# New inputs for a kernel's list planner: weight casts further behind landing, later weight parts, smaller transfer times, new tile offsets

## The chip, the cores and the metric

The kernel runs on one core of one Trainium2 chip. The metric is device time in microseconds, the median of several runs. The engines are called as the profile calls them: PE (TensorE matmul; PEld its weight loads), DVE (VectorE), ACT (ScalarE), POOL (GpSimd) and SP (SyncE, which here only issues DMAs).

## The reference

Retention-like attention for 8 batches, 8 heads, 576 positions and 64 values a head, then a mixture of 8 experts over its 4608 rows of 512 values, with a noisy gate that sends each row to two experts:

```python
scores = scale * np.matmul(q, k.transpose(0, 1, 3, 2))
ret = scores * Dmat[None]                      # gamma ** (i - j) for i >= j, else 0
x = np.matmul(ret, v)                          # then (B * S, H * D) = (4608, 512)
noisy_logits = x @ w_gate + np.log1p(np.exp(x @ w_noise)) * noise
top2 = np.argpartition(-noisy_logits, 2, axis=1)[:, :2]   # weights: softmax of the two
for e in range(8):
    for k in range(2):
        mask = top2[:, k] == e
        h = np.maximum(x[mask] @ w1[e], 0.0)   # 512 -> 1024
        out[mask] += top2_w[mask, k, None] * (h @ w2[e])   # 1024 -> 512
```

## The kernel before

**Attention** is worked in 16 units `u` (batch pairs `bp = u // 4`). After each batch pair `route` computes the gate, ranks the rows of each expert and builds a table of row numbers (`xi`), and the pair's rows are written to `xd` in DRAM.

**Expert tiles.** The rows of an expert come in groups `j` of 128, 9.5 groups for each. `tiles` makes 30 tiles `i`, each an expert `e`, a few groups `js`, and the batch pair `bp` after which it can be gathered. Tiles 0 to 10 are *early*: expert 0 to 3's first groups, gathered while attention still runs, up to 256 rows wide. Tiles 11 to 29 are *late* (`bp` is 3) and up to 512 rows wide: one for expert 0, two each for experts 1 to 3, three each for experts 4 to 7.

A tile passes through these operations:

- `fetch`: POOL gathers its rows from `xd` (L1246, `at="fetch1"`); the rows are transposed, late ones by DMA transposes that SP issues (L1258, `fetch2`), early ones and those of expert 3 by PE (L1268, `fetch3`) with a copy from PSUM on ACT or DVE (`fetch4`).
- `up` (early, L1328) or `wide` (late, L1354): x @ w1 on PE, and relus on ACT or DVE (L1337, L1339; `up1`, `wide1`, `wide2`).
- `down`: h @ w2 on PE (L1418 full groups, L1437 half groups). For late tiles these matmuls are put between those of the next tile's `wide`. The last tile's come after all else: the half group in one piece (`record2`), the full group in two columns (L1427, `record3`).
- `finish`: an eviction scaled by the gate (L1469, L1471, L1473; `finish2`, for the split last group `finish1`), then POOL scatters to `out`: rows whose first contribution it is (`finish3`, `first`), or that add to an earlier one (`finish4`, `second`; L1483). A few late groups read the earlier sum beforehand (`before`, L1514).

**Weights.** Expert 0 to 2's are loaded and cast to bf16 by POOL's DMAs. Expert 3 to 7's come in eight parts each (`part`): SP loads 512 KB of f32 into a `big` buffer (L1183, L1186), of which the planner allows this use four at a time, and ACT or DVE casts it to bf16 (helper line L459 or L461). `weights(e + 4)` is called in the last tile of expert `e`; it appends eight parts to a list, the k-th due `SPREAD[e] * k` steps later. A step is one of the eight blocks of a `wide`, so a late tile has eight steps. `due` takes parts from the front of the list only, so a part waits for all before it.

**What sets the order.** Each engine and queue runs its instructions in the order in which `Plan.run` emits them. `Plan` is a list planner: it gives every operation a start time from its own table of costs (`cost` on the engine, `dma` for a transfer, `hold` for a distance behind the landing of a DMA that the operation reads), and emits next the one with

```python
key = (round(t * 20), o.prio, o.i)
```

the smallest. So a priority decides only between operations that could start in the same twentieth of a planned microsecond; the smaller number goes first. Attention's operations have priorities of about `u` (up to some 17), tile `i` has `100 + 4 * i` (late gathers and transposes 8 less), expert 3's parts 60. To that, `op` adds an offset by the operation's name `at`:

```python
prio += ORDER[at][min(3, int(max(0.0, prio)) // 4) if prio < 60 else 4 if prio < 136 else 5]
```

Columns 0 to 3 of `ORDER` are attention's; column 4 is that of tiles 0 to 8 and expert 3's parts, column 5 that of everything later. The planned times are not used on the chip: there every instruction waits for what it reads.

Of the kernel before, what the change touches and what calls it, by code (L numbers as in the profile page):

```python
# [21 lines left out]
F = 1024  # L22
# [5 lines left out]
NH = E * HPE  # L28
FIRST = (1216, 1024, 855, 690, 526, 361, 197, 0)
WAIT = (10, 15, 15)  # L30
SPREAD = (0, 0, 0, 0, 3, 3, 4, 4)
PACE = 2.343
REST = (85.0, 200.0, 1.6)
AHEAD = (2, 3)
# [122 lines left out]
    "route48": (-0.5, -0.25, -1.5, 0, -0.5, -0.5),  # L157
    "route49": (2, 5, 0.5, -1.5, 2, 2),
    "route50": (-2.5, -2, -2, -6.5, -2.5, -2.5),
    "overflow_table1": (-2, -2, -2, -2, -2, -2),  # L160
    "overflow_table2": (-2, -2, -2, -2, -2, -2),
    "overflow_table3": (-0.25, -0.25, -0.25, -0.25, -0.25, -0.25),
    "overflow_table4": (-2, -2, -2, -2, -2, -2),
    "weights1": (-0.75, -0.75, -0.75, -0.75, -0.75, -0.75),
    "part1": (2, 2, 2, 2, 2, 2),
    "fetch1": (-5, -5, -5, -5, -6, -4),
    "fetch2": (-1.25, -1.25, -1.25, -1.25, -1.5, -2.25),
    "fetch3": (0.5, 0.5, 0.5, 0.5, -3, 1.5),
    "fetch4": (-0.25, -0.25, -0.25, -0.25, 0.75, 0.75),
    "fetch5": (0, 0, 0, 0, 0, -4),  # L170
    "fetch6": (-4, -4, -4, -4, -8.25, -1.5),
    "fetch7": (-1.25, -1.25, -1.25, -1.25, 6.5, -3.25),
    "fetch8": (-2.5, -2.5, -2.5, -2.5, -4, 0),
    "mix1": (0.25, 0.25, 0.25, 0.25, 0.25, 0.25),
    "mix2": (4, 4, 4, 4, 4, 4),
    "mix3": (2.25, 2.25, 2.25, 2.25, 2.25, 2.25),
    "up1": (2, 2, 2, 2, 2, 2),
    "wide1": (2.75, 2.75, 2.75, 2.75, 2.75, 2.75),
    "wide2": (1.25, 1.25, 1.25, 1.25, 1.25, 1.25),
    "finish1": (-2.25, -2.25, -2.25, -2.25, -2.25, -2.25),  # L180
    "finish2": (0, 0, 0, 0, 0, 5.5),
    "finish3": (5.75, 5.75, 5.75, 5.75, 24, 6.75),
    "finish4": (5.5, 5.5, 5.5, 5.5, 5.5, 5.5),
    "record1": (3, 3, 3, 3, 3, 3),
    "record2": (1.75, 1.75, 1.75, 1.75, 1.75, 1.75),
    "record3": (6.5, 6.5, 6.5, 6.5, 6.5, 6.5),
    "record4": (2, 2, 2, 2, 2, 2),
}
BIG = 1.0e6
NOV = NCOL * E  # L190
# [223 lines left out]
class Kernel:  # L414
# [762 lines left out]
    def part(self, e, k, prio, after):  # L1177
        pl, nc = self.pl, self.nc
        w, t = self.W[e], pl.buf("big", "exp")

        def ld(_):
            if k < KD:
                nc.sync.dma_start(out=t.t, in_=self.w1[e, k * P:(k + 1) * P, :])  # L1183
            else:
                fo = 2 * (k - KD)
                nc.sync.dma_start(out=t.t.rearrange("p (fo d) -> p fo d", fo=2),  # L1186
                                  in_=self.w2[e, fo * P:(fo + 2) * P, :].rearrange("(fo fi) d -> fi fo d", fi=P))
        pl.op("SP", 0.55, ld, w=[t], prio=prio, dma=1.35, after=after)
        pl.op({"ACT": 1.06, "DVE": 0.7}, 0, lambda g: self.copy(g, w.t[:, k * F:(k + 1) * F], t.t), hold=1,
              r=[t], w=[(w, k)], prio=prio, at="part1")  # L1190

    def tiles(self):
# [35 lines left out]
    def fetch(self, i, t, prio):  # L1228

        pl, nc = self.pl, self.nc  # L1230
        e, js, early = t
        ident = self.fixed["ident"]
        xi = self.fixed[f"xi{early}"]
# [3 lines left out]
        for x, j, two in zip(xg, js, joint):  # L1237
            if two:
                if e % 2:
                    continue  # L1240
                self.tailx[e] = x
            h, n = HPE * e + j, P
            pace = PACE if early == 3 and i > self.ne else 0.0

            def get(_, x=x, h=h, n=n, pace=pace):
                ins = nc.gpsimd.indirect_dma_start(  # L1246
                    out=x.t[:n, :], out_offset=None, in_=self.xd[:rows, :], in_offset=IOff(ap=xi.t[:n, h:h + 1], axis=0),
                    bounds_check=rows - 1, oob_is_err=False)
                if pace:
                    self.tc.add_manual_dep(ins.ins, self.mm.ins.name, mybir.DependencyInfo(  # L1250
                        mybir.DependencyClass.Sync, mybir.DependencyReason.DATA), reason="gathers go at TensorE's pace")
            self.got = pl.op("POOL", 1.3, get, r=[xi if two else (xi, "m")] + self.xd_done[early], w=[x], prio=prio, dma=0.4, pace=pace, slack=3, ind=True, at="fetch1")
        xT = pl.buf("half" if early < 3 else "big", "xt")
        w, m, off = sum(self.size(j) for j in js), len(js) * P, self.off(js)
        xv = lambda m=m: xT.t.bitcast(BF16)[:, :KD * m].rearrange("p (k s) -> p k s", k=KD)
        if early == 3 and e != 3:
            for s, x in enumerate(xg):
                pl.op("SP", 2.0, lambda _, s=s, x=x, n=self.size(js[s]), p=self.span(e, js[s]): nc.sync.dma_start_transpose(  # L1258
                    out=xv()[:, :, off[s]:off[s] + n], in_=x.t[p, :DM // 2].bitcast(BF16)),
                    r=[x], w=[(xT, s)], prio=prio, dma=1.1, hold=3, at="fetch2")  # L1260
        for c in range(0, 0 if early == 3 and e != 3 else len(js), 2):
            p = self.psum("xt")
            pv = lambda p=p: p.t.bitcast(BF16).rearrange("p (k s) -> p k s", k=KD)
# [10 lines left out]
        for x, j, two in zip(xg, js, joint):  # L1274
            k = self.kind(e, j)
            pay = lambda x=x: x.t[:, DM // 2:]
            if early == 3 and two and e % 2 and e < 2:
                c = pl.buf("pay", "exp")
                pl.op("DVE", 0.1, lambda _, x=x, c=c: self.nc.vector.tensor_copy(c.t[:HD], x.t[HD:, DM // 2:DM // 2 + 3]),
                      r=[x], w=[c], prio=prio, hold=3, at="fetch5")  # L1280
                pay, x = (lambda c=c: c.t), c
# [4 lines left out]
            else:  # L1286
                gm, im = self.fix(f"gm{e}", [P, 1]), self.fix(f"im{e}", [P, 2], I32)
                m, mb = self.mix(e)
# [158 lines left out]
    def finish(self, i, t, s, prio, split=False):  # L1447
# [43 lines left out]
        if first:  # L1491
            key = self.outk.setdefault(e, pl.fix())
            self.scats.setdefault(i, []).append(pl.op("POOL", 1.3, lambda _: scat(first, False), r=[y] + src, w=[(key, j)],
                                                      prio=prio, dma=0.76, ind=True, at="finish3"))
        if second:
            rd = [self.outk[x] for x in self.outk if x < e]
            self.scats.setdefault(i, []).append(pl.op("POOL", 1.3 if held else 1.8, lambda _: scat(second, not held),
                                                      r=[y] + src + rd, prio=prio, dma=0.9, after=self.reads if held else (), ind=True, at="finish4"))

    def before_it(self, e):  # L1500
        return [w for x in range(e) for w in self.firsts[x]]
# [1 line left out]
    def before(self, i, t, s, prio):  # L1503

        pl, nc, tc = self.pl, self.nc, self.tc
        e, js, _ = t
        q = self.span(e, js[s], 2)
        if self.size(js[s]) < P:
            q, e = slice(0, P), E - 1
        g, first, second, src = self.t[i]["gi"][s]  # L1510
        y = pl.buf("half", "ty")

        def get(_):
            ins = nc.gpsimd.indirect_dma_start(  # L1514
                out=y.t[q, :], out_offset=None, in_=self.out[:, :], in_offset=IOff(ap=second()[q], axis=0),
                bounds_check=N - 1, oob_is_err=False).ins
            tc.declare_no_dep(ins, group="scat", keep=self.before_it(e), reason="rows of out are disjoint or ordered by hand")
            tc.add_to_no_dep_group("scat", ins)
        self.reads.append(pl.op("POOL", 1.3, get, r=[src] + [self.outk[x] for x in self.outk if x < e], w=[y], prio=prio - 2, dma=0.9))
        self.t[i].setdefault("y", {})[s] = y  # L1520


# [226 lines left out]
```

## Time and profile before

| | |
|---|---|
| time, median of 3 runs | 411.0 us (410.47 to 411.59) |
| profiled execution | 412.69 us, span 411.1 us, granted clock 0.989 |
| busy: PE, ACT, POOL, DVE | 377.1, 272.3, 291.0, 148.2 us |
| DMA | 98.06 MB, mean 239 GB/s |
| gathers, transposes by DMA, scatters | 76, 55, 82 |

The span runs from the first to the last instruction of one profiled execution. A row of the timeline names start, duration, engine, line, operation, output and inputs, and in brackets how long the engine had been idle before it and what ended that. "issue" means that it waited for nothing that the profile shows. In the table of stretches each row has the length and then the busy time of PE, PEld, DVE, ACT and POOL, the granted clock of PE, the share of the DMA engines and GB/s. PE runs attention and the first early tiles up to about 149 us, the other early tiles to about 200 us, and the late tiles from there to 405.7 us.

### The profile page before, as it was taken

To read this page: it belongs to the slowest core of one execution; us is meant where nothing else is said; L and a number is where in the kernel's file an instruction comes from. 1 tells how busy PE (TensorE), PEld (TensorE's weight loads), DVE (VectorE), ACT (ScalarE), POOL (GpSimd) and SP (SyncE) were. 2 spreads that over 40 slices of the span, in tenths; PEclk is the share of its full clock that TensorE was granted. 3 is DMA by queue.
4 is the path that set the end of the run, shared out by engine and by line. 5 is a ranking of instruction groups with operands and counts; after the bars stand their busy time and mean duration, and the time that the engine had idled before them with its cause. 6 is when DMAs were issued, how large, how long until landed. Compare 5 with 4: busy or idle time off the path is not lost.

```text
span 411.1 us, 11031 instructions
## 1 busy us (share of the span) xinstructions
PE 377.1 (92%) x4320; PEld 233.3 (57%) x4320; DVE 148.2 (36%) x413; ACT 272.3 (66%) x468; POOL 291.0 (71%) x379
## 2 busy tenths in 40 slices
PE   4998867889898898999999999999999999999994
PEld 2567656677575666767556554544554454454453
DVE  8456798788269587220111322101011000000002
ACT  2589978898787765776555877666686445555451
POOL 8676783990799848778676477778675776728564
PEclk9899999989999999999999999999999999999999
DMA  8999998999999989999989899999999998839766
GB/s 226 290 298 255 317 305 254 306 269 252 275 286 205 264 188 284 395 246 221 280 188 377 288 331 223 260 251 230 296 257 211 165 202 152 164 45 133 127 94 131
DMA packets 106184, 98.06 MB, mean 239 GB/s; under 512 B 40975, under 2 KB 83472, under 8 KB 106130
## 3 DMA queue, kind: packets, MB, share of 16 engines
q1 hardware_dynamic: 85858, 60.92, 56.0%
q0 software_dynamic: 17584, 36.24, 43.4%
q8 instruction: 34, 0.56, 0.6%
q10 hardware_dynamic: 2688, 0.18, 0.4%
q14 instruction: 20, 0.16, 0.2%
HBM read 73.11 MB, written 26.10 MB: 241 GB/s over the span
## 4 chain that ended last, share of the span: by engine, by line
PE 65%; DVE 8%; POOL 7%; DMA 6%; issue 6%; ACT 6%; POOLq 0%; SPq 0%; another core or an unknown queue 0%; DVEq 0%; ACTq 0%
PE ps L1418 25%; PE ps L1354 23%; PE ps L1328 6%; POOL out_dram L1483 4%; DMA xd<-xg 2%; ACT half L459 2%; DMA half<-in_v_dram 2%; DVE half L783 2%; PE ps L1437 2%; PE ps L808 2%; PE ps L467 1%; POOL half L721 1%; ACT xT L459 1%; DVE olo L1074 1%; PE ps L1268 1%
## 5 line engine op out<-in xcount | busy, mean ns | idle before, releaser
L1337 ACT ACTIVATE half<-ps 128x512 bf16<-128x512 f32 (+5 forms) x184 | 90.6, 503 | 87.5 <-PE ps L1354 55.0
L1418 PE MATMUL ps<-W,half 128*128 128x512 bf16 x432 | 137.8, 379 | 1.4 <-issue 1.1
L1354 PE MATMUL ps<-big,W 128*128 128x512 bf16 (+4 forms) x448 | 124.5, 326 | 0.6 <-DVE half L1473 0.6
L1246 POOL DMA_INDIRECT xg<-xd,xi x76 | 79.1, 1040 | 48.2 <-DMA half<-in_v_dram 11.7
L1483 POOL DMA_INDIRECT out_dram<-half,xg x71 | 90.3, 1272 | 30.1 <-issue 14.8
L1418 PEld LDWEIGHTS <-half 128*128 128x128 bf16 x568 | 54.5, 98 | 62.8 <-issue 3.1
L1354 PEld LDWEIGHTS <-W 128*128 128x128 bf16 x448 | 43.8, 98 | 33.4 <-issue 0.8
L1354 PE MATMUL ps<-big,xT 128*128 128x512 bf16 (+2 forms) x160 | 47.6, 337 | 0.0
L1471 ACT ACTIVATE half<-ps,xg 128x512 f32<-128x512 f32 (+1 forms) x58 | 39.3, 678 | 10.0 <-PE ps L1418 6.7
L783 DVE TENSOR_TENSOR half<-ps,mask 128x512 bf16<-128x512 f32 x64 | 40.3, 682 | 14.3 <-PE ps L775 10.9
L1418 PE MATMUL ps<-xT,half 128*128 128x512 bf16 x136 | 44.9, 379 | 0.0
L459 ACT ACTIVATE half<-ps 128x1024 bf16<-128x1024 bf16 (+1 forms) x42 | 38.5, 946 | 7.9 <-PE ps L744 4.0
L1473 DVE TENSOR_SCALAR half<-ps,xg 128x512 f32<-128x512 f32 (+1 forms) x17 | 10.6, 623 | 76.8 <-PE ps L1437 42.0
L1328 PE MATMUL ps<-half,W 128*128 128x256 bf16 (+1 forms) x288 | 29.1, 255 | 1.6 <-DVE half L461 0.8
L1339 DVE TENSOR_SCALAR half<-ps 128x512 bf16<-128x512 f32 (+5 forms) x12 | 6.8, 569 | 60.5 <-issue 32.9
L1328 PEld LDWEIGHTS <-W 128*128 128x128 bf16 x288 | 23.7, 98 | 5.8 <-issue 1.8
L467 PE MATMUL ps<-mask,ident__61 128*128 128x512 bf16 x68 | 20.3, 429 | 3.7 <-DVE hpf L527 3.7
L1469 DVE SCALAR_TENSOR_TENSOR half<-ps,xg,half 64x256 f32<-64x256 f32 (+2 forms) x7 | 3.6, 521 | 55.2 <-PE ps L1437 32.4
L1354 PEld LDWEIGHTS <-xT 128*128 128x128 bf16 x160 | 15.6, 98 | 12.8 <-issue 0.4
L459 ACT ACTIVATE tb<-ps 64x512 bf16<-64x512 f32 x32 | 18.9, 591 | 4.0 <-POOL half L721 1.9
L459 ACT ACTIVATE W<-big 128x1024 bf16<-128x1024 f32 x20 | 21.0, 1059 | 0.0
L808 PE MATMUL ps<-half,half 64*64 64x64 bf16 (+2 forms) x512 | 17.2, 213 | 1.7 <-ACT xT L459 1.6
(204 smaller groups left out, 517.0 us busy)
## 6 DMA issues: line engine op xcount, KB each, us to landing
big<-in_moe_w_dram SPq DMA_DIRECT2D x40, 512.0 KB
W<-in_moe_w_dram POOLq DMA_DIRECT2D x12, 512.0 KB
xd<-xg SPq DMA_DIRECT2D x16, 264.0 KB
W<-in_q_dram SPq DMA_DIRECT2D x16, 256.0 KB
big<-in_k_dram SPq DMA_DIRECT2D x8, 512.0 KB
big<-in_v_dram SPq DMA_DIRECT2D x8, 512.0 KB
big<-in_q_dram SPq DMA_DIRECT2D x16, 256.0 KB
W<-in_k_dram SPq DMA_DIRECT2D x6, 512.0 KB
```

The source lines that it names most:

```text
L459: self.nc.scalar.activation(out, in_, Act.Copy)
L467: self.nc.tensor.matmul(b.t, lhsT=ident, rhs=mask.rearrange("p r x -> p (r x)").unsqueeze(1).to_broadcast([P, 2, 2 * P]), start=True, stop ...
L783: nc.vector.tensor_tensor(S.t.bitcast(BF16).rearrange("p (h c x) -> p h c x", h=2, c=2)[:, h], p[h].t.rearrange("p (c x) -> p c x", c=2), ...
L808: nc.tensor.matmul(o[h * HD:(h + 1) * HD, hp, n, :], lhsT=kk[:k, r, c, y], rhs=vv[:k, r, c, y].unsqueeze(1).to_broadcast([k, n.stop - n.st ...
L1246: ins = nc.gpsimd.indirect_dma_start(out=x.t[:n, :], out_offset=None, in_=self.xd[:rows, :], in_offset=IOff(ap=xi.t[:n, h:h + 1], axis=0), ...
L1328: nc.tensor.matmul(pv()[:, f2, :], lhsT=w.t[:, o:o + P], rhs=xv()[:, di, :n], start=(di == 0), stop=(di == KD - 1))
L1337: self.nc.scalar.activation(o, i, Act.Relu)
L1354: self.mm = nc.tensor.matmul(p.t[:, :n], lhsT=w.t[:, o:o + P], rhs=xv()[:, di, :n], start=(di == 0), stop=(di == KD - 1))
L1418: self.mm = self.nc.tensor.matmul(po.t, lhsT=hv[:, c:c + P], rhs=self.W[e].t[:, o:o + DM], start=(f == 0), stop=(f == KF - 1))
L1471: nc.scalar.activation(y.t[q, c], x, Act.Copy, scale=g()[q])
L1473: nc.vector.tensor_scalar(y.t[q, c], x, g()[q], None, Alu.mult)
L1483: ins = nc.gpsimd.indirect_dma_start(out=self.out[:, :], out_offset=IOff(ap=ix()[q2], axis=0), in_=y.t[q2, :], in_offset=None, bounds_chec ...
```

## The change

Four kinds of edits, none of which adds or removes an instruction:

- `part`: the cast of a part of experts 4 to 7 has `hold=6`, not 1.
- `SPREAD` for experts 4 to 7: 4, 5, 6, 7 steps from part to part, not 3, 3, 4, 4.
- Transfer times of late operations in the planner: gathers 0.3 (0.4), DMA transposes 0.55 (1.1), scatters 0.55 (0.76) and 0.6 or 1.2 (0.9), reads 0.6 (0.9).
- Columns 4 and 5 of `ORDER` for nearly all tile operations.

```diff
-SPREAD = (0, 0, 0, 0, 3, 3, 4, 4)
+SPREAD = (0, 0, 0, 0, 4,5,6,7)
...
-    "part1": (2, 2, 2, 2, 2, 2),
-    "fetch1": (-5, -5, -5, -5, -6, -4),
-    "fetch2": (-1.25, -1.25, -1.25, -1.25, -1.5, -2.25),
-    "fetch3": (0.5, 0.5, 0.5, 0.5, -3, 1.5),
-    "fetch4": (-0.25, -0.25, -0.25, -0.25, 0.75, 0.75),
+    "part1": (2, 2, 2, 2, 197.5, 100.25),
+    "fetch1": (-5, -5, -5, -5, 2.25, -1.75),
+    "fetch2": (-1.25, -1.25, -1.25, -1.25, -86.5, -57.75),
+    "fetch3": (0.5, 0.5, 0.5, 0.5, -73.25, -107.5),
+    "fetch4": (-0.25, -0.25, -0.25, -0.25, -90.5, -66.25),
...
-    "up1": (2, 2, 2, 2, 2, 2),
-    "wide1": (2.75, 2.75, 2.75, 2.75, 2.75, 2.75),
-    "wide2": (1.25, 1.25, 1.25, 1.25, 1.25, 1.25),
-    "finish1": (-2.25, -2.25, -2.25, -2.25, -2.25, -2.25),
-    "finish2": (0, 0, 0, 0, 0, 5.5),
-    "finish3": (5.75, 5.75, 5.75, 5.75, 24, 6.75),
-    "finish4": (5.5, 5.5, 5.5, 5.5, 5.5, 5.5),
-    "record1": (3, 3, 3, 3, 3, 3),
-    "record2": (1.75, 1.75, 1.75, 1.75, 1.75, 1.75),
-    "record3": (6.5, 6.5, 6.5, 6.5, 6.5, 6.5),
+    "up1": (2, 2, 2, 2, -254.75, -8.5),
+    "wide1": (2.75, 2.75, 2.75, 2.75, 21, 62.25),
+    "wide2": (1.25, 1.25, 1.25, 1.25, 16, -6),
+    "finish1": (-2.25, -2.25, -2.25, -2.25, -47, -24.5),
+    "finish2": (0, 0, 0, 0, -77, -4.75),
+    "finish3": (5.75, 5.75, 5.75, 5.75, 96.75, -164),
+    "finish4": (5.5, 5.5, 5.5, 5.5, 0.75, -57.75),
+    "record1": (3, 3, 3, 3, -86.5, -152),
+    "record2": (1.75, 1.75, 1.75, 1.75, 26.5, 82.5),
+    "record3": (6.5, 6.5, 6.5, 6.5, -53, -145),
...
-        pl.op({"ACT": 1.06, "DVE": 0.7}, 0, lambda g: self.copy(g, w.t[:, k * F:(k + 1) * F], t.t), hold=1,
+        pl.op({"ACT": 1.06, "DVE": 0.7}, 0, lambda g: self.copy(g, w.t[:, k * F:(k + 1) * F], t.t), hold=6 if e > 3 else 1,
...
-            self.got = pl.op("POOL", 1.3, get, r=[xi if two else (xi, "m")] + self.xd_done[early], w=[x], prio=prio, dma=0.4, pace=pace, slack=3, ind=True, at="fetch1")
+            self.got = pl.op("POOL", 1.3, get, r=[xi if two else (xi, "m")] + self.xd_done[early], w=[x], prio=prio, dma=0.3 if early == 3 else 0.4, pace=pace, slack=3, ind=True, at="fetch1")
...
-                    r=[x], w=[(xT, s)], prio=prio, dma=1.1, hold=3, at="fetch2")
+                    r=[x], w=[(xT, s)], prio=prio, dma=0.55, hold=3, at="fetch2")
...
-                                                      prio=prio, dma=0.76, ind=True, at="finish3"))
+                                                      prio=prio, dma=0.55 if t[2] == 3 else 0.76, ind=True, at="finish3"))
-                                                      r=[y] + src + rd, prio=prio, dma=0.9, after=self.reads if held else (), ind=True, at="finish4"))
+                                                      r=[y] + src + rd, prio=prio, dma=0.9 if t[2] < 3 else 0.6 if held else 1.2, after=self.reads if held else (), ind=True, at="finish4"))
...
-        self.reads.append(pl.op("POOL", 1.3, get, r=[src] + [self.outk[x] for x in self.outk if x < e], w=[y], prio=prio - 2, dma=0.9))
+        self.reads.append(pl.op("POOL", 1.3, get, r=[src] + [self.outk[x] for x in self.outk if x < e], w=[y], prio=prio - 2, dma=0.6))
```

More of the change, by code (lines that the diff above doesn't have):

```diff
@@ L159 @@
     "route50": (-2.5, -2, -2, -6.5, -2.5, -2.5),
[L160 to L163, printed above, removed]
+    "overflow_table1": (-2, -2, -2, -2, 41.75, -10.25),
+    "overflow_table2": (-2, -2, -2, -2, 1.75, -63.25),
+    "overflow_table3": (-0.25, -0.25, -0.25, -0.25, 13, -10.75),
+    "overflow_table4": (-2, -2, -2, -2, -104, -32),
@@ L164 @@
     "weights1": (-0.75, -0.75, -0.75, -0.75, -0.75, -0.75),
-    "part1": (2, 2, 2, 2, 2, 2),
-    "fetch1": (-5, -5, -5, -5, -6, -4),
-    "fetch2": (-1.25, -1.25, -1.25, -1.25, -1.5, -2.25),
-    "fetch3": (0.5, 0.5, 0.5, 0.5, -3, 1.5),
-    "fetch4": (-0.25, -0.25, -0.25, -0.25, 0.75, 0.75),
[L170 to L174, printed above, removed]
@@ L175 @@
-    "mix2": (4, 4, 4, 4, 4, 4),
-    "mix3": (2.25, 2.25, 2.25, 2.25, 2.25, 2.25),
-    "up1": (2, 2, 2, 2, 2, 2),
-    "wide1": (2.75, 2.75, 2.75, 2.75, 2.75, 2.75),
-    "wide2": (1.25, 1.25, 1.25, 1.25, 1.25, 1.25),
-    "finish1": (-2.25, -2.25, -2.25, -2.25, -2.25, -2.25),
-    "finish2": (0, 0, 0, 0, 0, 5.5),
-    "finish3": (5.75, 5.75, 5.75, 5.75, 24, 6.75),
-    "finish4": (5.5, 5.5, 5.5, 5.5, 5.5, 5.5),
-    "record1": (3, 3, 3, 3, 3, 3),
-    "record2": (1.75, 1.75, 1.75, 1.75, 1.75, 1.75),
@@ L186 @@
-    "record3": (6.5, 6.5, 6.5, 6.5, 6.5, 6.5),
-    "record4": (2, 2, 2, 2, 2, 2),
+    "part1": (2, 2, 2, 2, 197.5, 100.25),
[3 more added lines that the diff above has]
+    "fetch4": (-0.25, -0.25, -0.25, -0.25, -90.5, -66.25),
+    "fetch5": (0, 0, 0, 0, 69, 143.75),
+    "fetch6": (-4, -4, -4, -4, -65, 18.5),
+    "fetch7": (-1.25, -1.25, -1.25, -1.25, 40.25, -41.75),
+    "fetch8": (-2.5, -2.5, -2.5, -2.5, 6.75, -55.5),
@@ new lines @@
+    "mix1": (0.25, 0.25, 0.25, 0.25, -10, 29),
+    "mix2": (4, 4, 4, 4, -124.25, 18.5),
+    "mix3": (2.25, 2.25, 2.25, 2.25, -28, 18),
+    "up1": (2, 2, 2, 2, -254.75, -8.5),
[6 more added lines that the diff above has]
+    "record1": (3, 3, 3, 3, -86.5, -152),
@@ L188 @@
+    "record2": (1.75, 1.75, 1.75, 1.75, 26.5, 82.5),
+    "record3": (6.5, 6.5, 6.5, 6.5, -53, -145),
+    "record4": (2, 2, 2, 2, -83.75, -63.5),
 }
```

## The prediction

> **What bounds the kernel now.** I read the page first (busy time, slices), then the table of stretches, then the TensorE timeline around each hole, and last SyncE's queue and the tail.
>
> ```profile
> span 411.1 us, 11031 instructions
> PE 377.1 (92%) x4320; PEld 233.3 (57%) x4320; DVE 148.2 (36%) x413; ACT 272.3 (66%) x468; POOL 291.0 (71%) x379
> ...
> PE   4998867889898898999999999999999999999994
> ...
> q8 instruction: 34, 0.56, 0.6%
> ```
> ```profile
> 100.00:140.00 40.00, 34.37 (x688) 24.46 (x686) 25.14 (x66) 31.27 (x54) 32.84 (x38) 1.00 1.09 256
> 140.00:160.00 20.00, 19.20 (x265) 15.12 (x263) 15.25 (x54) 14.60 (x29) 13.26 (x23) 1.00 0.95 210
> 160.00:180.00 20.00, 18.40 (x156) 12.35 (x153) 5.87 (x14) 12.28 (x19) 15.54 (x23) 1.00 1.12 357
> 180.00:200.00 20.00, 19.77 (x175) 13.43 (x173) 1.02 (x2) 12.28 (x22) 16.45 (x26) 1.00 0.99 242
> ...
> 220.00:240.00 20.00, 19.35 (x150) 11.91 (x148) 5.23 (x13) 14.22 (x26) 12.03 (x12) 1.00 0.93 335
> ...
> 300.00:320.00 20.00, 20.00 (x112) 9.76 (x110) 3.05 (x9) 13.45 (x22) 13.93 (x11) 1.00 1.27 208
> ```
>
> TensorE (PE, the second figure of a row) is idle 5.63 us between 100 and 140, while attention still runs. From 140 on, where the experts are nearly alone, it is idle 0.80, 1.60, 0.23 and 0.65 us in the four stretches shown, 3.28 us together, and nothing in a stretch like 300 to 320. Is a busy PE also a PE at full rate? The starts say so:
>
> ```profile
> 295.72 0.38 PE L1418 MATMUL ps<-W,half 128*128 128x512 bf16 x1
> 295.94 0.25 PE L1354 MATMUL ps<-big,W 128*128 128x192 bf16 x1
> 296.02 0.38 PE L1418 MATMUL ps<-W,half 128*128 128x512 bf16 x1
> ```
>
> 512 columns take 0.22 us from start to start, 192 take 0.08: 704 columns in 0.30 us, with a granted clock of 1.00 in the rows above. Nothing that only orders work can shorten that. So all the change can win after 140 is those 3.28 us and something of the tail; all it can lose is a new wait.
>
> **Which holes depend on the order.**
>
> ```profile
> 114.68 1.03 PE L1328 MATMUL ps<-half,W 128*128 128x256 bf16 x8 [0.46 <-DVE half L461]
> 163.59 2.33 PE L1418 MATMUL ps<-W,half 128*128 128x512 bf16 x10 [1.11 <-issue]
> 170.54 3.65 PE L1328 MATMUL ps<-half,W 128*128 128x256 bf16 x32 [0.37 <-DVE half L461]
> 188.95 0.61 PE L1418 MATMUL ps<-W,half 128*128 128x512 bf16 x2 [0.15 <-ACT half L1337]
> 229.91 0.32 PE L1354 MATMUL ps<-big,W 128*128 128x384 bf16 x1 [0.65 <-DVE half L1473]
> ```
> ```profile
> 162.93 0.60 ACT L1337 ACTIVATE half<-ps 128x512 bf16<-128x512 f32 x1 [2.64 <-remote]
> 229.11 0.75 DVE L1473 TENSOR_SCALAR half<-ps,xg 128x512 f32<-128x512 f32 x1 [9.53 <-PE ps L1354]
> ```
>
> The bracket gives PE's idle time and what ended it. Two holes (0.46 and 0.37) end with the copy of a tile's transposed tokens, one (0.15) with a relu, one (0.65) with an eviction: in these an order could help, 1.63 us in all. The 1.11 is different: the relu behind it started at 162.93 after ScalarE had stood idle 2.64 us, released by nothing of this kernel that the profile names. A queue with nothing in it can't be put in a better order, so I count that hole as staying. The Trainium skill ("Runtime: NRT & Kernel Launch", Instruction fetch mechanics) says engines fetch instructions in 16 KiB blocks on a DMA queue of their own and that this is mostly hidden; the q8 row, 0.56 MB in 34 packets, agrees on the block size. Hidden fetches would leave the kernel's own order as the cause, so by that rule the hole could close too; that case stands among the rivals.
>
> **The change part by part.** No instruction is added or removed. It gives the planner other inputs: (a) weight casts of experts 4 to 7 may be planned only 6 us after their landing, not 1; (b) their eight parts each come every 4, 5, 6 and 7 steps, not 3, 3, 4, 4; (c) smaller transfer times for the late gathers, transposes, scatters and reads; (d) offsets that decide between operations that could start at the same planned time.
>
> (a) and (b). The casts:
>
> ```profile
> L459 ACT ACTIVATE W<-big x20: 1045/1048/1114, 216.3 to 285.8; 128x1024 bf16<-128x1024 f32 x20
> L461 DVE CAST W<-big x4: 683/690/693, 206.4 to 252.8; 128x1024 bf16<-128x1024 f32 x4
> ```
>
> The same casts, about 1.05 us each on ScalarE, fall later and further apart and lose their ties (+100.25), and ScalarE is at most 14.22 of 20 us busy in the late rows above. Are the weights still in time? Eight steps make one late tile. Parts leave one first-in-first-out list, so expert 4's go at steps 0 to 28, expert 5's at 28 to 51, 6's at 51 to 74, 7's at 74 to 97. Expert 4's last is issued at step 28, in the fourth late tile (starts 226.50), and first used at step 56; expert 7's at step 97, in the thirteenth (326.94), and used at step 128.
>
> ```profile
> 226.50 0.33 PE L1354 MATMUL ps<-big,W 128*128 128x384 bf16 x1
> ...
> 268.57 0.38 PE L1354 MATMUL ps<-big,W 128*128 128x512 bf16 x1
> ...
> 326.94 0.25 PE L1354 MATMUL ps<-big,W 128*128 128x192 bf16 x1
> ...
> 369.58 0.38 PE L1354 MATMUL ps<-big,xT 128*128 128x512 bf16 x1
> ```
>
> Somewhat under 268.57 - 226.50 = 42 and 369.58 - 326.94 = 43 us remain; landing plus 6 us plus a cast fit. Cost 0. The cover would be gone only with 35 us of delay. What is bought: the eviction behind the 0.65 us hole shares its stretch with casts that now move later. Bounds -0.65 to 0; I take -0.65, and a hole of the 0.15 kind could be next.
>
> (c) A gather planned 0.1/0.85 = 0.12 us shorter and a transpose 0.55/0.95 = 0.58 us shorter put what follows earlier in the queues. SyncE then stands at a transpose whose gather hasn't landed; queued behind it are weight loads and the next transposes:
>
> ```profile
> SPq L1258 <- DMA xg<-xd,xi: 36.1, 18, 7.5
> SPq L1183 <- PE ps L1354: 10.3, 1, 10.3
> ```
> ```profile
> 286.83 15.70 SPq L1258 DMA_TRANSPOSE big<-xg  x4
> 302.62 1.05 SPq L1186 DMA_DIRECT2D big<-in_moe_w_dram  x2
> ```
> ```profile
> 313.12 0.39 PE L1354 MATMUL ps<-big,W 128*128 128x512 bf16 x1
> ```
>
> It does so now, 36.1 us in 18 waits, and PE sees none of it: even the closest tile, with transposes issued by 302.53, is begun at 313.12, 10.6 us later. Cost 0 while the queue slips by less than that. The scatters' and reads' new sizes move POOL's queue only; cost 0 by the full 300 to 320 row of PE.
>
> (d) Relus of the early tiles (-254.75) and copies of their transposed tokens (-90.5) now win nearly every tie on ScalarE and VectorE, and their PE transposes (-73.25) win against matmuls of other tiles. That speaks to 0.46, 0.37 and 0.15 us: -0.98, bounds -0.98 to 0. The price is paid by attention, which loses those ties. Its nearest row:
>
> ```profile
> L1337 ACT ACTIVATE half<-ps 128x512 bf16<-128x512 f32 x8 | 4.4, 616 | 0.1
> ```
>
> Eight relus before 141, 4.4 us, if every one held attention up. But ScalarE has 40 - 31.27 = 8.73 us idle from 100 to 140, and from 140 on PE has expert work whatever attention does. I take 0, with +4.4 as the end. Casts of expert 3's parts (+197.5) and early scatters (+96.75) lose their ties instead; both engines have room (12.28 and 15.54 of 20), cost 0. On PE itself expert 3's late transposes (-107.5) move ahead of matmuls; they stay planned 5 us behind their gathers' landing, cost 0. POOL's late scatters now win against gathers:
>
> ```profile
> L1483 POOL DMA_INDIRECT out_dram<-half,xg x71 | 90.3, 1272 | 30.1 <-issue 14.8
> ```
>
> A gather behind one or two of them comes 1.3 to 2.5 us later, against the 10.6 above, cost 0.
>
> The tail. The short last piece (now +82.5) and the two column pieces of the last tile (-145) wait for the same relus; so far the short one went first (1.75 against 6.5), now the columns do.
>
> ```profile
> 402.77 1.06 PE L1437 MATMUL ps<-xT,half 128*64 128x256 bf16 x16
> ...
> 403.76 1.92 PE L1427 MATMUL ps<-xT,half 128*128 128x256 bf16 x16
> 403.90 1.04 POOL L1483 DMA_INDIRECT out_dram<-half,xg  x1 [0.85 <-DVE half L1469]
> 403.94 1.50 DVE L1469 SCALAR_TENSOR_TENSOR half<-ps,xg,half 64x256 f32<-64x256 f32 x3 [0.32 <-PE ps L1437]
> 405.24 1.02 POOL L1483 DMA_INDIRECT out_dram<-half,xg  x1 [0.30 <-DVE half L1469]
> 405.79 0.48 DVE L1469 SCALAR_TENSOR_TENSOR half<-ps,xg,half 128x256 f32<-128x256 f32 x1 [0.34 <-issue]
> 406.57 0.99 POOL L1483 DMA_INDIRECT out_dram<-half,xg  x1 [0.31 <-issue]
> ```
>
> PE ends at 405.68 either way. Now one eviction of 0.48 us follows, then the last scatter at 406.57. With the short piece last two of 0.50 us follow: 405.68 + 0.11 (as from 403.83 to 403.94) + 1.00 + 0.30 (as from 406.27 to 406.57) = 407.09, +0.52 us. Bounds 0 (the second column has no PSUM buffer yet) to +0.52; I take +0.52.
>
> Sum: -0.65 - 0.98 + 0.52 = -1.11 us. The profiled execution took 412.69 us (span 411.1 and 1.6 around it), 1.7 above the 411.0 median; on the median that makes 409.9.
>
> **The rivals.** One: attention gains as well. If the new order of the mixed stretch also fills a third of the 5.63 us idle before 140, 1.9 us go: 408.0. For it: the 0.46 us hole at 114.68 shows that tile work there waits for copies which now go first. Against: only ties move, and attention's own offsets are untouched.
>
> Two: the change doesn't do what it says. The plan shifts, the holes reappear beside other instructions, as a hole that no queue explains may: 411.0, or 411.5 with the tail.
>
> Three, slower: a block at the head of SyncE's queue. Step 56 begins at 268.57 and step 88 at 313.12, so step 74 lies near 294 us; there expert 6's last and four of expert 7's parts come due together. The load that finds no free buffer waits for a cast, and casts are now planned 5 us later: the 10.3 us wait of the row above becomes 15.3. If transposes of the tile begun at 313.12 stand behind it, PE waits 15.3 - 10.6 = 4.7 us: 411.0 + 4.7 - 1.1 = 414.6; with less behind it, 412.5 to 414. It decides from 10.6 us on. Against: the transposes have a lower number than those loads (-57.75) and win ties.
>
> Four: the 1.11 us hole at 163.59 hung on the order after all, and the new one closes it as well: -1.11 - 1.11, 408.8. Against it stands the idle ScalarE of the 162.93 row. This is what the Trainium skill's rule of hidden fetches, named above, would make of it.
>
> **How the numbers follow.** A difference of 0.3%, 1.2 us, is about what a measurement of this kernel can tell from none. The forecast, holes of the order closing and the tail giving some back, 409.9 (own range 409.0 to 411.0), has 0.40; since it lies near the bound I put 0.17 of that to faster and 0.23 to no difference. Rival one 0.15 (faster), rival two 0.15 (same), rival three 0.22 (slower), rival four 0.08 (faster). Faster 0.40, same 0.38, slower 0.22. With 0.1 left out at either end, and attention's +4.4 not added to rival three, the range goes from 407.6 to 413.0.
>
> **What would show it.** Right: PE idle from 140 to 240 under 2.2 us, no copy of transposed tokens named before a PE hole, PE all busy from 240 to 400, the columns before the short piece at the end and the last scatter about 0.5 us further behind PE's end. Wrong: a PE hole behind a weight cast or transposed tile after 240; more idle time between 100 and 140; a hole ended by "issue" that goes away.

## The result, and the profile after

The changed kernel takes 407.88 us (median of 14 runs, 406.48 to 410.36), the kernel before in the same series 411.13 us (14 runs, 408.01 to 414.93). The ratio is 0.9926, with a 95% interval of 0.9905 to 0.9947: 3.25 us less. The profiled execution took 407.64 us (span 405.9); that of before, 412.69 us, lies 1.56 us above its median of this series, so about a third of the 5.2 us between the two spans is that execution's own. Ratios here and below leave out runs more than 1.5% above the fastest of their kernel; some experiments lose most runs by that, so their runs are listed too.

The page after, busy times and the slices of PE:

```profile
span 405.9 us, 11028 instructions
...
PE 376.1 (93%) x4324; PEld 235.1 (58%) x4324; DVE 146.5 (36%) x408; ACT 272.2 (67%) x474; POOL 290.7 (72%) x375
...
PE   5897977778989989999999999999999999999994
```

The four more matmuls are fillers (L467, 72 against 68) that the planner puts where it expects PE to wait, so the change does add a few instructions on PE.

The table of stretches after, for the same stretches as before (length, then busy time of PE, PEld, DVE, ACT and POOL, the granted clock, the DMA share, GB/s):

```profile
100.00:140.00 40.00, 38.26 (x748) 29.85 (x746) 28.61 (x75) 33.34 (x58) 32.82 (x38) 1.00 1.11 261
140.00:160.00 20.00, 18.16 (x275) 13.26 (x272) 13.19 (x47) 14.16 (x28) 12.64 (x21) 1.00 0.94 224
160.00:180.00 20.00, 19.78 (x180) 14.10 (x179) 8.75 (x20) 14.53 (x24) 16.87 (x25) 1.00 1.08 341
180.00:200.00 20.00, 20.00 (x160) 12.85 (x159) 2.29 (x7) 11.19 (x21) 17.32 (x25) 1.00 1.09 252
...
220.00:240.00 20.00, 20.00 (x145) 12.02 (x143) 4.77 (x11) 14.46 (x29) 14.66 (x14) 1.00 1.02 279
240.00:400.00 160.00, 160.00 (x907) 81.30 (x904) 11.11 (x30) 97.84 (x175) 110.55 (x88) 1.00 1.05 197
```

PE's idle time fell from 5.63 to 1.74 us between 100 and 140 (-3.89), rose from 0.80 to 1.84 between 140 and 160 (+1.04), and fell from 2.48 to 0.22 between 160 and 240 (-2.26). Before 100 it is 1.0 us more, after 240 it is nothing in both. With 1.0 us less busy time that makes the 5.1 us by which PE ends earlier (405.68 to 400.60).

PE's order in the two kernels first differs at about 93 us, so the mixed stretch is better taken as a whole. From 85 to 160 us, before and after:

```profile
85.00:160.00 75.00, 67.45 (x1264) 51.11 (x1258) 54.18 (x144) 59.23 (x103) 54.49 (x74) 0.98 1.06 243
```
```profile
85.00:160.00 75.00, 69.27 (x1303) 53.69 (x1303) 55.14 (x148) 59.49 (x104) 54.07 (x73) 0.98 1.07 249
```

Idle time there fell from 7.55 to 5.73 us. So 1.8 us of the 3.89 remain; the rest is given back on both sides. The prediction had given this part 0.46 us.

What filled it? PE's timeline of before, its longest hole first, then around 140; then the same of after:

```profile
108.91 0.62 PE L893 MATMUL ps<-ident__61,half 128*128 128x128 bf16 x8 [1.62 <-POOL half L881]
...
132.75 0.24 PE L775 MATMUL ps<-half,half 64*64 64x128 bf16 x2 [0.81 <-ACT xT L459]
...
139.55 0.30 PE L843 MATMUL ps<-half,half 64*64 64x128 bf16 x6 [1.16 <-issue]
...
141.16 1.04 PE L1328 MATMUL ps<-half,W 128*128 128x256 bf16 x8
...
148.61 0.22 PE L1030 MATMUL ps<-MM,ltri 128*128 128x144 bf16 x1 [0.46 <-DVE MM L1003]
```
```profile
132.43 1.91 PE L1328 MATMUL ps<-half,W 128*128 128x256 bf16 x16
...
135.07 1.91 PE L1328 MATMUL ps<-half,W 128*128 128x256 bf16 x16
...
137.59 0.31 PE L908 MATMUL ps<-half 64*64 64x64 bf16 x14 [0.46 <-DVE oh L1076]
...
145.43 0.60 PE L1418 MATMUL ps<-W,half 128*128 128x512 bf16 x2 [1.24 <-issue]
...
152.41 0.24 PE L1030 MATMUL ps<-MM,ltri 128*128 128x144 bf16 x1 [0.60 <-DVE MM L1003]
```

L1328 is the first layer of tile 2, expert 1's first two groups: 32 matmuls of 256 rows. Before, they ran from 141.16 on, and in PE's instruction order not one of attention's score and value matmuls (L744 to L934) came after them. After, they run from 132.43 to 137, with 180 attention matmuls still to come. They take places in which PE waited for attention's copies, such as the 0.81 us at 132.75. The 1.62 us at 108.91 is another matter: two kernels below (the planner's numbers alone and column 5 alone) have PE's order of before up to about 180 us and no such hole there, so it belonged to this execution and not to the order. Attention itself ends later for it: its last ranking (L1030) starts at 152.41, not 148.61. So attention had 3.8 us to spare, since PE has expert work from there on; what counted was that ready expert work stood behind it in PE's queue.

The end of the kernel, after:

```profile
397.68 1.06 PE L1437 MATMUL ps<-xT,half 128*64 128x256 bf16 x16
...
398.68 1.92 PE L1427 MATMUL ps<-xT,half 128*128 128x256 bf16 x16
...
400.71 0.48 DVE L1469 SCALAR_TENSOR_TENSOR half<-ps,xg,half 128x256 f32<-128x256 f32 x1 [0.35 <-PEq L1638]
401.48 0.99 POOL L1483 DMA_INDIRECT out_dram<-half,xg  x1 [0.31 <-DVE half L1469]
```

The short piece (L1437) still goes first, and the last scatter starts 0.88 us after PE's end, 0.89 before. The tail has not changed.

### The profile page after: what moved, and what is told of

Same layout as the page of the kernel before. It is cut to its first block, busy times and chain, and to the rows that moved or that the text cites. A ratio compares the mean times of both kernels' runs of the same rounds, so it can differ in the third digit from the quotient of the medians.

```text
span 405.9 us, 11028 instructions
## 1 busy us (share of the span) xinstructions
PE 376.1 (93%) x4324; PEld 235.1 (58%) x4324; DVE 146.5 (36%) x408; ACT 272.2 (67%) x474; POOL 290.7 (72%) x375
## 5 line engine op out<-in xcount | busy, mean ns | idle before, releaser
L1337 ACT ACTIVATE half<-ps 128x512 bf16<-128x512 f32 (+5 forms) x192 | 94.3, 502 | 73.5 <-PE ps L1354 58.7
L1246 POOL DMA_INDIRECT xg<-xd,xi x76 | 80.6, 1060 | 46.5 <-DMA half<-in_v_dram 11.0
L1471 ACT ACTIVATE half<-ps,xg 128x512 f32<-128x512 f32 x62 | 42.6, 687 | 13.0 <-PE ps L1418 12.6
L459 ACT ACTIVATE half<-ps 128x1024 bf16<-128x1024 bf16 (+1 forms) x43 | 39.6, 950 | 7.9 <-DMA noise<-in_moe_noise_dram 2.9
L1473 DVE TENSOR_SCALAR half<-ps,xg 64x256 f32<-64x256 f32 (+1 forms) x13 | 7.1, 544 | 89.6 <-PE ps L1437 45.3
L1328 PE MATMUL ps<-half,W 128*128 128x256 bf16 (+1 forms) x288 | 29.3, 255 | 0.1
L1328 PEld LDWEIGHTS <-W 128*128 128x128 bf16 x288 | 23.9, 98 | 3.2 <-issue 0.2
L467 PE MATMUL ps<-mask,ident__61 128*128 128x512 bf16 x72 | 20.6, 416 | 3.7 <-DVE hpf L527 3.7
L459 ACT ACTIVATE xT<-big 128x1024 bf16<-128x1024 f32 x13 | 13.7, 1053 | 7.8 <-DMA big<-in_moe_w_dram 7.8
L459 ACT ACTIVATE W<-big 128x1024 bf16<-128x1024 f32 x17 | 17.9, 1053 | 0.0
L459 ACT ACTIVATE xg<-ps 128x1024 bf16<-128x1024 bf16 (+1 forms) x18 | 16.2, 936 | 2.5 <-PE ps L1110 1.2
```

What stands on the lines that cost most here:

```text
L459: self.nc.scalar.activation(out, in_, Act.Copy)
L467: self.nc.tensor.matmul(b.t, lhsT=ident, rhs=mask.rearrange("p r x -> p (r x)").unsqueeze(1).to_broadcast([P, 2, 2 * P]), start=True, stop ...
L1246: ins = nc.gpsimd.indirect_dma_start(out=x.t[:n, :], out_offset=None, in_=self.xd[:rows, :], in_offset=IOff(ap=xi.t[:n, h:h + 1], axis=0), ...
L1328: nc.tensor.matmul(pv()[:, f2, :], lhsT=w.t[:, o:o + P], rhs=xv()[:, di, :n], start=(di == 0), stop=(di == KD - 1))
L1337: self.nc.scalar.activation(o, i, Act.Relu)
L1471: nc.scalar.activation(y.t[q, c], x, Act.Copy, scale=g()[q])
```

## The experiments

The first four ran on one chip, where the kernel before took 411.55 us (23 runs).

**All offsets, none of the planner's numbers.**

```diff
 ORDER = (as changed)
-SPREAD = (0, 0, 0, 0, 4,5,6,7)
+SPREAD = (0, 0, 0, 0, 3, 3, 4, 4)
-hold=6 if e > 3 else 1
+hold=1        # and the transfer times as before
```

> The new offsets in both columns; casts, steps and transfer sizes as before. Theory one (the early tiles' new ranks among attention's operations bring matmuls of the next tile into TensorE's holes from 100 to 140 us): TensorE idle in that stretch 1.7 us as after the change, not 5.6, and 0.9 of the whole gain or more, 407.5 to 409. Theory two (the planner's new numbers for casts, steps and transfers take the holes of 160 to 240 us away): those stay at 2.5 us, and the gain is halved, 409 to 410.

Measured: one run at 406.96 us, five from 415.25 to 422.66. Stretches, and PE's waits after 165, of a profiled execution of 422.66 us:

```profile
100.00:140.00 40.00, 37.17 (x668) 28.62 (x665) 29.08 (x67) 32.18 (x56) 29.27 (x35) 1.00 1.04 242
...
240.00:400.00 160.00, 151.30 (x818) 74.76 (x817) 13.02 (x31) 87.33 (x158) 104.49 (x84) 0.97 0.99 183
```
```profile
PE ps L1354 <- DMA big<-xg: 6.5, 1, 6.5
PE ps L1437 <- ACT half L1337: 1.7, 1, 1.7
```

Idle time before 140 is lower (2.83), but from 85 to 160 it is 7.90 us in this profile, no less than before; 8.7 us are lost after 240, where neither of the two kernels loses anything. The holes from 160 to 240 are gone (0.21 us idle) without the planner's numbers, so the second theory of the expectation falls.

**The planner's numbers, no offset.**

```diff
 SPREAD, hold and transfer times as changed
-ORDER = (as changed)
+ORDER = (as before)
```

> The new cast distance, steps and transfer sizes with all offsets as before. Theory one: 100 to 140 us as before (idle 5.6), time within 1 us of before. Theory two: 160 to 240 us loses about 2 us of idle time, time 408.5 to 409.5. Should the loss by a blocked SyncE queue exist, it would show here: over 412.

Measured: 411.30 us (12 runs, 409.62 to 414.38), ratio 1.0002 (0.9972 to 1.0032).

```profile
100.00:140.00 40.00, 35.45 (x748) 26.39 (x747) 27.08 (x71) 32.02 (x56) 33.65 (x39) 1.00 1.11 263
...
160.00:180.00 20.00, 18.90 (x171) 13.21 (x169) 5.77 (x16) 13.67 (x20) 16.86 (x27) 1.00 1.08 367
```

By themselves the numbers are worth nothing that these runs can tell: 4.55 us idle before 140, 1.10 between 160 and 180. All of the 1.10 is one wait for a relu (175.51); the hole of before at 163.59 isn't there, though PE's order up to it is the same.

**Column 4 alone** (tiles 0 to 8 and expert 3's parts) **and column 5 alone** (later tiles).

```diff
 ORDER[at][4] as changed, all else as before     # column 4 alone
 ORDER[at][5] as changed, all else as before     # column 5 alone
```

> Only column 4 of the offsets is new (early tiles 0 to 8, expert 3's parts). Theory one: idle of 100 to 140 us at 1.7, nearly the whole gain, 407.5 to 409. Theory two: at most half of it, 409 to 411.

> Only column 5 of the offsets is new (tiles 9 and later). Both theories: idle of 100 to 140 us as before at 5.6, and TensorE fully busy from 240 on as before, since it had nothing to wait for there: within 1 us of before. The short last piece is still ahead of the columns.

Measured: column 4 alone 406.43, 407.23 and 408.78 us in three runs and 413.27, 413.39 and 414.03 in three; ratio of the first three 0.989 (0.9826 to 0.9954). Column 5 alone 412.98 us (12 runs, 408.5 to 418.29), ratio 1.0012 (0.9976 to 1.0047). Stretches of column 4 alone, then of column 5 alone:

```profile
100.00:140.00 40.00, 38.65 (x694) 29.23 (x693) 27.07 (x69) 33.78 (x58) 31.81 (x37) 0.97 1.07 252
...
160.00:180.00 20.00, 19.78 (x172) 13.71 (x170) 9.25 (x19) 13.84 (x23) 16.39 (x26) 1.00 1.10 350
```
```profile
100.00:140.00 40.00, 35.68 (x755) 26.47 (x752) 25.93 (x69) 31.95 (x56) 33.98 (x40) 1.00 1.10 255
```

By its three shorter runs column 4 carries the gain, 160 to 180 included (from 85 to 160 it is idle 6.56 us); no profile shows what lengthens the other three. Column 5 alone was expected to lose nothing after 240, but in its profile (a run of 416.92 us) PE is idle 4.66 us there. The PE order of column 4 alone is that of the changed kernel up to about 163 us. The order that other offsets would give says which of them do it: with the offsets of `fetch3`, `fetch4` and `up1` (early tiles' PE transposes, their copies, their relus) tile 2's first layer comes before attention's end, and with any of the three left out it stands behind all attention matmuls again; with `record1` it starts and ends where the changed kernel has it. That is read from instruction orders; the next two kernels try it on a chip.

They and the next two ran on another chip, where the kernel before takes 420.11 us (13 runs).

**These four offsets with the planner's numbers; and the changed kernel without `up1`'s.**

```diff
 ORDER: column 4 as changed for fetch3, fetch4, up1, record1 alone; SPREAD, hold, sizes as changed
```
```diff
-    "up1": (2, 2, 2, 2, -254.75, -8.5),
+    "up1": (2, 2, 2, 2, 2, -8.5),
```

> Before, with the new cast distance, steps and transfer sizes, and of all new offsets only four: column 4 of fetch3, fetch4, up1 and record1. These put the matmuls of tile 2's first layer 180 attention matmuls ahead of attention's end in TensorE's program instead of behind it, as the whole change does. Theory one (that is the gain): idle from 100 to 140 us 1.3 to 2.2, time 407 to 409. Rival (the gain needs the offsets of column 5 or the other names): idle as after but time within 1 us of before, 410 to 412.

> The whole change except the offset of the early tiles' relus (up1, column 4, back to 2). Tile 2's first layer then stands behind all attention matmuls again. Theory one: idle from 100 to 140 us back at 4.5 to 5.6, time 409.5 to 411.5. Rival (many small ties, no single one matters): 407.5 to 409.

Measured: the four offsets 409.69, 409.88 and 410.89 us in three runs and 417.92, 419.36 and 421.24 in three; ratio of the first three 0.9749 (0.9664 to 0.9834). Without `up1` 417.10 us (10 runs, 413.50 to 425.52), ratio 0.9909 (0.9864 to 0.9953), against 0.9813 (0.9766 to 0.9861) of the changed kernel on that chip, below. The stretch without `up1`:

```profile
100.00:140.00 40.00, 35.11 (x723) 25.74 (x723) 26.27 (x70) 29.65 (x53) 32.74 (x38) 1.00 1.08 253
```

One number of column 4 takes the idle time before 140 back to 4.89 us, as in the two kernels without column 4 (4.55, 4.32). That is 1.75 us more than the changed kernel has there (3.14, below). Taken up to 160 us it is 25.2 against 24.4, only 0.9 us more, because this execution was idle 2.9 us less up to 85 us, where the orders are the same. The times differ by more than that (no run below 413.50); the rest of it isn't placed. The four offsets are idle 3.44 us before 140 in the profile below, more than the 1.3 to 2.2 expected, with tile 2's first layer at 132.60.

What do the long runs of the four offsets show? SyncE's queue, ScalarE and PE in the profile of the run of 419.36 us:

```profile
306.19 18.23 SPq L1258 DMA_TRANSPOSE big<-xg  x4
324.51 1.09 SPq L1186 DMA_DIRECT2D big<-in_moe_w_dram  x2
```
```profile
324.78 0.60 ACT L1337 ACTIVATE half<-ps 128x512 bf16<-128x512 f32 x1
332.43 1.06 ACT L459 ACTIVATE xT<-big 128x1024 bf16<-128x1024 f32 x1 [7.05 <-DMA big<-in_moe_w_dram]
333.39 0.58 ACT L1337 ACTIVATE half<-ps 128x512 bf16<-128x512 f32 x1
```
```profile
334.03 0.61 PE L1418 MATMUL ps<-W,half 128*128 128x512 bf16 x1 [6.49 <-ACT half L1337]
```

Read it downwards. SyncE stands for 18 us at four transposes; behind them stand two weight loads, issued at 324.51. Their casts are in ScalarE's queue at a place where the planner thought them landed, and the first waits 7.05 us for it; its load lands 7.9 us after its issue. The relu behind that cast has its input, but waits too, and PE waits 6.49 us for the relu. No short run of this kernel was profiled, so that this hole is what makes its long runs long is a conclusion, not a comparison.

**The cast distance and the spread undone, one at a time.**

```diff
-hold=6 if e > 3 else 1
+hold=1
```
```diff
-SPREAD = (0, 0, 0, 0, 4,5,6,7)
+SPREAD = (0, 0, 0, 0, 3, 3, 4, 4)
```

> The whole change except the cast distance (hold 1 for all). Theory one (with the new order a cast planned 1 us behind its landing stands in ScalarE's queue before relus, and TensorE waits, as in the profile of the offsets alone): TensorE idle 2 to 9 us from 240 on in the profile, or in some runs, time 409 to 418. Rival (the steps between parts are what protects): no idle after 240, 407 to 409.

> The whole change except the steps (3, 3, 4, 4 as before). Theory one (the cast distance protects): no idle after 240, 407 to 409. Rival: the parts come in closer bunches, SyncE's queue blocks transposes, and TensorE is idle 2 to 9 us after 240, 409 to 418.

Measured: old distance 414.41 us (4 runs, 411.84 to 415.32), ratio 0.9845 (0.9768 to 0.9921); old spread 411.99 us (4 runs, 410.94 to 413.59), ratio 0.9793 (0.9726 to 0.9861). PE's largest hole after 240, with the old distance and with the old spread:

```profile
327.13 0.38 PE L1354 MATMUL ps<-big,W 128*128 128x512 bf16 x1 [1.39 <-ACT half L1337]
```
```profile
284.01 0.39 PE L1418 MATMUL ps<-W,half 128*128 128x512 bf16 x1 [3.09 <-ACT half L1337]
```

Both show the late hole in small, but without the changed kernel beside them they can't say how much it costs. So these ran together, on the same chip (before: 419.03 us, 8 runs):

> The changed kernel once more, for comparison with the two after it on the same chip. Theory: idle from 100 to 140 us 1.5 to 2.5, no or one short hole after 240 us, ratio to before 0.975 to 0.993.

> The same kernel as after_hold1 (cast distance back to 1 us), now beside the whole change. Theory one (the cast distance is the guard): 2 us or more slower than the whole change in the same call, with holes after 240 us behind a relu on ScalarE or a landing. Rival (steps and sizes suffice): within 1 us of it.

> All of column 4 and all new planner numbers, column 5 of the offsets as before. Theory one (column 5 gives nothing of its own, the gain is column 4's): within 1 us of the whole change. Rival (column 5 was fitted to the new numbers and keeps late holes away): 2 us or more slower than it, with holes after 240 us.

The third is column 4 and all the planner's numbers, with column 5 as before. Measured: the changed kernel 409.84 us (5 runs, 409.19 to 413.32), ratio 0.9813 (0.9766 to 0.9861); with the old cast distance 410.87 us (5 runs, 409.44 to 415.32), ratio 0.982 (0.9762 to 0.9878); with the old column 5 409.16, 411.64, 415.08, 420.30 and 421.58 us, ratio of the first three 0.9831 (0.9766 to 0.9897). Stretches of the changed kernel on this chip, then of the old distance, then of the old column 5:

```profile
100.00:140.00 40.00, 36.86 (x726) 27.71 (x725) 27.64 (x73) 30.89 (x53) 33.49 (x39) 1.00 1.12 262
...
240.00:400.00 160.00, 158.60 (x876) 80.51 (x893) 9.59 (x27) 98.51 (x178) 110.94 (x88) 1.00 1.02 201
```
```profile
240.00:400.00 160.00, 158.48 (x868) 80.22 (x883) 10.93 (x28) 97.31 (x177) 112.96 (x90) 1.00 0.97 200
```
```profile
240.00:400.00 160.00, 155.95 (x841) 78.43 (x854) 14.91 (x35) 96.59 (x166) 108.38 (x87) 0.99 1.01 200
```

The changed kernel is idle 3.14 us before 140 here, more than the 1.5 to 2.5 expected (1.74 on the first chip). The profiles of this chip hold 34 or 35 matmul records fewer than weight loads (4290 and 4324 in the first of them), so part of the idle time that they show, above all after 160 us, is missing records.

The old distance loses nothing that these runs can tell (1.0 us between medians, intervals on top of each other): that the distance of 6 us guards the gain is not shown, and my theory that it does falls. Without column 5 the hole behind a late cast is back (3.21 us at 334.86 in the run of 420.30).

**PE's instructions shifted.** 64 small matmuls (32 columns each) stand ahead of PE's first fill, so that all later PE instructions lie 128 places further on (line numbers are 4 higher).

```diff
+        if not getattr(self, "shifted", False):
+            self.shifted = True
+            for _ in range(64):
+                self.nc.tensor.matmul(b.t[:, :32], lhsT=ident, rhs=ident[:, :32], start=True, stop=True, skip_group_check=True)
```

> The whole change with 64 small matmuls (32 columns, 128 instructions with their weight loads) more on TensorE at its first wait, which shift every later instruction by half of a 256-instruction block. Theory (the holes of about 1 us that end in issue are TensorE waiting for its next block of instructions): in the changed kernel's places, such as the one inside the second layer's matmuls near 144 us, the hole is gone, others of 0.8 us or more have come elsewhere, and each begins 0.2 to 2 us after a packet of the instruction queue. Rival (they belong to the place in the program): the hole near 144 us, moved by what the additions cost, stays at the same matmul. The additions themselves cost 2 to 6 us.

Measured: one run, 423.71 us. Most of its loss is the late hole once more (whether the shift brought it on, one run can't tell), its ScalarE row first; the third row is the one that the experiment was for:

```profile
335.82 1.06 ACT L459 ACTIVATE xT<-big 128x1024 bf16<-128x1024 f32 x1 [7.81 <-DMA big<-in_moe_w_dram]
```
```profile
337.41 0.61 PE L1422 MATMUL ps<-W,half 128*128 128x512 bf16 x1 [8.79 <-ACT half L1341]
```
```profile
144.87 0.36 PE L847 MATMUL ps<-half,half 64*64 64x128 bf16 x12 [0.77 <-issue]
```

The changed kernel has its "issue" hole of 1.24 us between second-layer matmuls (145.43, above). With the shift there is none between those; attention's L847 has one, and it is the matmul that now has the same number counted from the start of the program (see the last section). As a measure of what the shift costs, the run is inconclusive.

## Why the prediction was right, and where its steps failed

The forecast was 409.9, within 407.6 to 413.0, and faster the likeliest; 407.88 came, 0.28 us above the lower bound. The sum holds only part of the gain: the holes that it closes closed, and rival one, for which I had 408.0, came on top, with the hole that I had counted as staying. That 408.0 lies so near is luck: its 1.9 us was a guessed third, and it still holds the hole that went and the tail's 0.52 us that didn't come.

**Attention's price, taken as 0, was a gain. This is the step that failed.** I read the 5.63 us before 140 as attention's own waiting and asked only what attention would lose when the tiles' relus and copies go first. The row to read was 141.16, PE's first expert matmuls behind the last attention matmul: the tile's rows could have been ready nine microseconds sooner, and PE stood idle between. Between 100 and 140 the two profiles differ by 3.9 us, from 85 to 160 by 1.8 us, about what rival one named (1.9 of 5.63 us). How much of that is the order is known only roughly: the two kernels with the order of before are idle 8.00 and 7.98 us from 85 to 160, before itself 7.55; column 4 alone 6.56, all offsets 7.90. By these profiles it is between nothing and 2 us. What I had said against rival one, that attention's own offsets are untouched, doesn't matter: attention ends 3.8 us later. The 0.46 us of the sum also lie in this stretch, so rival one counted them twice in part.

**The holes that an order closes** (-0.65 and -0.98): all four are gone. No copy of a transposed tile stands before a hole from 100 on, 220 to 240 is full, and idle time from 140 to 240 is 2.06 us, under the 2.2 named. My cause for the 0.65 was the casts' distance; the planner's numbers alone close it, but so do column 4 alone and column 5 alone (0.02, 0.09 and 0 us idle from 180 to 240, against 0.88), so the cause isn't told apart, and the 160 to 180 part needs column 4 (1.10 idle without, 0.22 with).

**The 1.11 us hole "that stays"** went, which the prediction named as a sign against it. That doesn't show rival four's reason, the order: the planner's numbers alone and column 5 alone keep PE's order of before up to there and don't have the hole either. Its matmuls began 0.06 us after the end of the late relu that the prediction showed (162.93 + 0.60 = 163.53). What held ScalarE for 2.64 us stays open.

**The tail, +0.52, measured 0.** The planner hands out these PSUM buffers in the order in which the operations were recorded. The short piece is recorded first and has the first PSUM buffer, so no offset can put the columns ahead. That was the lower bound of this term.

**Casts and queues at cost 0:** right for the whole change, wrong for its parts. Rival three had the right place, SyncE's queue standing at transposes with weight loads behind them, and, but for one kernel, the wrong victim: with all offsets and the old numbers PE did wait 6.5 us for a transposed tile, in the others for a relu or an eviction behind a cast on ScalarE. Some ten microseconds of margin at the transposes were no margin for the casts. The changed kernel comes near it: its ScalarE also waits for a weight part, without PE noticing.

```profile
338.44 1.06 ACT L459 ACTIVATE xT<-big 128x1024 bf16<-128x1024 f32 x1 [4.08 <-DMA big<-in_moe_w_dram]
339.40 3.02 ACT L1337 ACTIVATE half<-ps 128x512 bf16<-128x512 f32 x6
```

After 240 no such wait is listed in the profiles of before and of the planner's numbers alone, nor in three of the other chip (the changed kernel, without `up1`, the second of the old distance). The longest is 2.4 us in column 4's, 4.1 here, 4.2 with all offsets, 3.3 and 4.4 with the old spread and in the first profile of the old distance (holes of 3.09 and 1.39), and 5.1, 7.1, 7.3 and 7.8 where PE lost 3.2, 6.5, 3.0 and 8.8 us. Column 4 and column 5 each bring it near or over that edge. That column 5 and the planner's numbers together keep the whole change on the good side is shown as a sum: none of its runs lies far off (14 within 3.9 us). Which of the numbers does it is open: distance and spread by themselves showed no loss beyond the spread of the runs, and the transfer times alone weren't tried.

By the median of all its runs no part of the change beat the whole. Column 4 alone reached 406.43, but half of its runs lie above 413.

## What to carry to other kernels

Idle time of the bounding engine in a stretch of mixed work belongs to nobody: ask first which ready work stands behind it in the queue, and whether the work in front has time to spare at its own end. Count what was won from the first place where the orders differ, since a hole that closes in one stretch can open in the next. Where a cast or copy that depends on a DMA shares an in-order engine with the work that feeds the bounding engine, its margin is the distance from landing to that place in the queue; measure it in the profile (here the wait of the cast for its weights), not by the margin of what the transfer is finally for. And where an order sits near such an edge, one short execution proves little: look at how all runs lie.

## What the runs showed of the hardware

**PE's "issue" holes follow the instruction queue's packets.** Over the profiles of all these kernels there are, after the first 15 us, 51 holes ended by "issue" where matmuls start 0.8 us or more later than their columns take; 48 of them opened 0.2 to 2.1 us after a packet of the instruction queue (q8, 34 or 35 packets of 16 KB in a run). From 20 to 200 us, where nearly all of them lie, the changed kernel has 23 packets; 23 windows of 1.9 us in 180 hold a quarter of such holes by chance. In the changed kernel one is recorded at 143.05, and the hole that ends at 145.43 opens at 144.19.

The places are more regular than that. Each matmul has one weight load; counted by these, 47 of the 51 holes lie within four matmuls of number 351 or of one that is a multiple of 128 further on (chance would put about 7 in 100 there). PE's weight loads begun by the end of a hole, for two holes of the changed kernel and one of the shifted:

```profile
0.00:118.79 118.79, 73.32 (x2140) 0.97 1.05 280
0.00:145.43 145.43, 92.79 (x2651) 0.98 1.06 273
```
```profile
0.00:144.87 144.87, 92.69 (x2651) 0.98 1.06 271
```

From 2140 to 2651 it is four times 128, less one; the hole of before that ends at 139.55 is at 2523, 128 ahead of 2651. Nine of the 14 profiles have a hole at 2651. With 64 matmuls put in front, half of 128, number 2651 is attention's L847 and not a second-layer matmul, and the hole stays at the number: it belongs to a place in PE's program, not to an operation. The program's 4324 matmuls and as many weight loads over 34 packets are 254 a packet. That a missing block of instructions is what PE waits for is a conclusion from this, not a measurement. The four holes elsewhere, that of before at 163.59 among them, lie after 160 us at second-layer matmuls; three of them end 0.05 or 0.06 us after a relu.

The 48 cost 0.8 to 2.3 us each; the changed kernel has six, all before 146 us, the kernel before two, the kernel without `up1` none. The Trainium skill ("Runtime: NRT & Kernel Launch", Instruction fetch mechanics) has the blocks, 16 KiB and 256 instructions, with which the trace agrees (128 matmuls with their weight loads), and calls the cost of crossing from one to the next mostly hidden. That holds here too: between 20 and 200 us the 14 profiles have 323 packets for these 48 holes.

**A late hole can cost more than its length.** The granted clock after the 8.79 us hole of the shifted kernel, and after the 1.69 us hole of column 5 alone:

```profile
337.40:341.00 3.60, 3.59 (x13) 1.88 (x14) 0.00 (x0) 2.83 (x6) 2.48 (x2) 0.50 1.27 239
...
343.00:350.00 7.00, 6.95 (x41) 3.72 (x41) 0.00 (x0) 3.88 (x10) 5.21 (x4) 1.00 1.14 178
```
```profile
281.90:285.00 3.10, 3.07 (x14) 1.31 (x15) 0.75 (x1) 1.56 (x4) 2.05 (x2) 1.00 1.08 322
```

After the long hole PE ran at 0.50 for about 4 us, some 2 us of work; after the short one at 1.00. Length alone doesn't decide: over the 3 us after holes of 2.97 us (column 5 alone, 305.90), 3.21 us (column 4 with the numbers, 334.86) and 3.09 us (old spread, 284.01) the clock was 0.67, 0.59 and 1.00, and after one of 1.66 us among attention's work (the numbers alone, 138.96) it was 0.51 from 140.5 to 144.0. The Trainium skill ("TensorE: Matmul & The Clock Gate", Part 1: The HAM clock gate) gives about 3.4 us as the idle window behind which the clock halves. The traces agree for holes of 6.5 and 8.8 us (0.50); here shorter ones lowered it too, so by these traces a hole under that length is not safe.

**The same kernel differs from chip to chip, and so does the gain.** The kernel before took 411.1 and 411.6 us in the first two series and 419.0 and 420.1 on the other chip; the changed kernel 407.9 and 409.8. The gain is 0.7% by the first (0.53 to 0.95%) and 1.9% by the second (1.4 to 2.3%). The late stream of matmuls accounts for little of it: 158.60 of 160 us busy there, in a stretch without a hole over 0.5 us, where the first profile has 160.00, and part of that is missing records (876 matmuls against 893 weight loads in that row, 907 against 904 in the first). The kernel before has no profile on the other chip, so what makes up the rest stays open.
